# Decode attention beside a gated MLP on one core: dealing the lanes of the key and value tiles by run and then by head

## The chip, the cores and the metric

The kernel runs on one core of a Trainium2 chip. The metric is the device time of one execution in microseconds (us); lower is better. TensorE (PE in the profile, PEld its weight loads), VectorE (DVE), ScalarE (ACT) and GpSimd (POOL) compute, SyncE (SP) issues the large transfers, and sixteen DMA engines move the data from memory (HBM) into SBUF, which has 128 partitions, here also called lanes.

## The reference

One decode step for four sequences: a layer norm, an attention over a cache of 4096 keys for each of 32 heads, and a gated MLP from the same normalized input, all added to the input. Cut to what matters (the helpers that only transpose are left out):

```python
# x: (4, 1, 640); k_cache, v_cache: (4, 32, 4096, 128); wq: (640, 4096); wo: (4096, 640), all bf16
xn = _layernorm(x)
q = (xn @ wq).reshape(B, Sq, Hq, Dh)          # then (b, h, q, d)
scores = einsum('bhqd,bhkd->bhqk', q, k_cache) * Dh ** (-0.5)
p = softmax(scores)
o = einsum('bhqk,bhkd->bhqd', p, v_cache)
attn = o.reshape(B, Sq, Hq * Dh) @ wo
# gated MLP: z = gelu(xn @ w_in), halves z1 and layernorm(z2), gate from w_sp and b_sp, then @ w_out
return x + attn + mlp
```

Keys and values of one head of one sequence are 4096 x 128 values of 2 bytes, 1 MB that lies in one piece in memory.

## The kernel before

The work is cut into NT = 16 tiles: tile i is eight heads (HT = 8, head group hg = i // 4) of one sequence b = i % 4. Its keys are 8 MB that lie in one piece in memory, and its values are another 8 MB. `run_view` (line 113) deals such a piece over the 128 lanes in order: each lane holds a run of NC = 256 consecutive keys, 64 KB, and since a head has 4096 keys, LN = 16 neighbouring lanes hold one head. So lane 16 h + l holds run l of head h, and lane p starts 64 KB after lane p - 1.

`load_k` (line 134) and `load_v` (line 141) issue the transfers on SP's queue into a ring of five units of 32 KB per lane. A key tile comes as one transfer of 64 KB per lane (the first as two of 32 KB), values as transfers of one or two units, and the last unit of values in smaller cuts. The order of all loads is a list written out by hand (`plan_k`, `plan_v`, `plan_wo`), and `pump` issues the next load as soon as the instructions that read the units it overwrites have been issued; SP then waits for these readers.

For each key tile and each quarter of it, VectorE multiplies keys with the query that was spread over the lanes (`product`, line 525), folds the halves (`fold`, line 541), TensorE adds up slices through an identity matrix (`sums`, line 550), and VectorE finishes the row sums (line 564). `lane_max` (line 573) needs the maximum over a head, that is over the lanes that hold it: it lays each lane's maximum into a column by its run number (`lane_diag`) and lets a matmul with `head_scale` add up over the lanes of one head. `exps` takes the exponentials, and `deal` (line 598) writes for every lane eight copies of its probabilities, each multiplied by one column of `hmask`, so that only the copy of the lane's own head is not zero. `blocks` (line 623) multiplies them with the values, adding over all lanes; `gather` (line 641) adds the blocks up. After four tiles a head group is divided by its sums (`group_den`, `group_rden`, `group_norm`) and projected by wo (`group_turn`, `group_pick`, `group_proj`). `group_turn` moves the result into rows in which wo was loaded, and `group_pick` (line 701) selects by a mask.

The masks are built once at the start from a 128 x 128 identity (`ident_f`, line 227): `lane_diag` (line 233), `hmask` (240), `head_scale` (247), and `q_lanes` (273), which spreads a query row over the lanes of its head; `place` (289) is sixteen small GpSimd copies that put query heads in order. They stand ahead of the stretch in which the engines' order is the order of the code (`manual_schedule`, line 732).

Of the kernel before, what the change touches and what calls it, by code (L numbers as in the profile page):

```python
# [9 lines left out]
FP32 = mybir.dt.float32  # L10
BF16 = mybir.dt.bfloat16
ACT = mybir.ActivationFunctionType
ALU = mybir.AluOpType
AX = mybir.AxisListType
# [6 lines left out]
def kernel(  # L21
# [14 lines left out]
    nc = tc.nc  # L36
    P = nc.NUM_PARTITIONS
    Bsz, Sq, D = A_x.shape
    _, H, S, Dh = A_k_cache.shape
# [8 lines left out]
    HT = 8  # L48
    HG = H // HT
    NT = HG * Bsz  # L50
    LN = P // HT
    NC = HT * S // P
# [23 lines left out]
    const = ctx.enter_context(tc.tile_pool(name="const", bufs=1))  # L76
# [11 lines left out]
    def units(first, n=1):  # L88
        return ring[:, first * UNIT : (first + n) * UNIT]
# [6 lines left out]
    def pair(i):  # L96
        if i in (0, NT - 1):
            return 2 if i == 0 else V_PAIR
        return 1 if i % 2 == 0 else 0
# [12 lines left out]

    def run_view(cache, i):
        hg, b = divmod(i, Bsz)
        return cache[b, HT * hg : HT * (hg + 1)].rearrange("h s d -> (h s) d").rearrange(
            "(p c) d -> p (c d)", c=NC
        )

    w_sb = units(W_UNIT)
    w_in_sb = w_sb[:, 0 : DC * F].rearrange("p (c n) -> p c n", c=DC)  # L120
# [13 lines left out]
    def load_k(i):  # L134
        t = units(pair(i), 2)
        step = (1 if i == 0 else 2) * UNIT
        for e in reversed(range(0, 2 * UNIT, step)):
            nc.sync.dma_start(out=t[:, e : e + step], in_=run_view(A_k_cache, i)[:, e : e + step])
        k_tiles[i] = t.rearrange("p (c d) -> p c d", d=Dh)

    def load_v(i, part, unit, n):
        t = units(unit, n)
        cuts = V_CUTS if (i, part) == (NT - 1, 1) else (0, n * UC)
        for c0, c1 in zip(cuts, cuts[1:]):
            src = slice((part * UC + c0) * Dh, (part * UC + c1) * Dh)
            nc.sync.dma_start(out=t[:, c0 * Dh : c1 * Dh], in_=run_view(A_v_cache, i)[:, src])
        for e in range(n):
            v_tiles[i, part + e] = units(unit + e).rearrange("p (c d) -> p c d", d=Dh)

# [20 lines left out]
    def plan_k(i):  # L170
        plan(("k", i), pair(i), 2, load_k, i)

    def plan_v(i, part, unit, n=1):
        plan(("v", i, part), unit, n, load_v, i, part, unit, n)
# [28 lines left out]
    def pump():  # L203
        while loads:
# [21 lines left out]
    ident_f = const.tile([P, P], FP32)  # L226
# [5 lines left out]
    lane_diag = const.tile([P, LN], FP32)  # L232
    nc.vector.tensor_reduce(
        out=lane_diag[:],
        in_=ident_f[:].rearrange("p (h l) -> p l h", h=HT),
        axis=AX.X,
        op=ALU.add,
    )
    hmask = const.tile([P, HT], FP32)
    nc.vector.tensor_reduce(  # L240
        out=hmask[:],
        in_=ident_f[:].rearrange("p (h l) -> p h l", h=HT),
        axis=AX.X,
        op=ALU.add,
    )
    head_scale = const.tile([P, P], FP32)
    nc.vector.tensor_scalar(
        out=head_scale[:].rearrange("p (h l) -> p h l", h=HT),
        in0=hmask[:, :, None].to_broadcast([P, HT, LN]),
        scalar1=scale_qk,  # L250
        scalar2=None,
        op0=ALU.mult,
# [7 lines left out]
        out=sel[:],  # L260
        in_=ident_f[:].rearrange("p (g h k) -> p k h g", g=CG, k=GC),
        axis=AX.X,
        op=ALU.add,
# [3 lines left out]
        out=spread[:],  # L267
        in_=ident[:].rearrange("p (m r) -> p r m", r=HT)[:, :, None, :].to_broadcast(
            [P, HT, HT, LN]
        ),  # L270
    )
    q_lanes = const.tile([HT * Bsz, Bsz, P], BF16)
    nc.vector.tensor_copy(
        out=q_lanes[:].rearrange("r b (h l) -> r b h l", h=HT),
        in_=ident[: HT * Bsz, : HT * Bsz]
        .rearrange("r (h b) -> r b h", b=Bsz)[:, :, :, None]
        .to_broadcast([HT * Bsz, Bsz, HT, LN]),
# [2 lines left out]
    QW = CW  # L280
    QH = HT // 2
    NQG = H // QH
    place = const.tile([P, QH, HT * Bsz], BF16)
    nc.gpsimd.memset(place[:], 0.0)
    for g in range(CG):
        ps = slice(g * QW, (g + 1) * QW)
        for hh in range(QH):
            at_col = (g % 2 * QH + hh) * Bsz
            nc.gpsimd.tensor_copy(
                out=place[ps, hh, at_col : at_col + Bsz], in_=lane_diag[ps, 0:Bsz]  # L290
            )

    hmask_bf = const.tile([P, HT], BF16)
# [9 lines left out]
    for i in range(NSTAT):  # L303
# [5 lines left out]
        out=rstd[:], in_=mv[:, 1:2], func=ACT.Sqrt, bias=eps_tile[:Bsz], scale=1.0  # L309
# [4 lines left out]
        out=xn_bf[:],  # L314
        in0=x_bf[:],
# [8 lines left out]
    for c in range(DC):  # L324
        nc.tensor.transpose(  # L325
            out=xnT_ps[:, c, :], in_=xn_v[:, c, :], identity=ident[:Bsz, :Bsz]
# [11 lines left out]
    for c in range(DC):  # L338
        for hg in range(NQG):
            g = hg % CG  # L340
            nc.tensor.matmul(  # L341
                out=q_ps[hg // CG][g * QW : (g + 1) * QW, :],
# [11 lines left out]
    def out_sum(half):  # L354
        return out_ps[OG * half : OG * half + Bsz, :]

    for half in range(2):
        nc.tensor.matmul(
            out=out_sum(half),
# [339 lines left out]
    def group_pick(hg):  # L699
        own = work.tile([P, HT, HT, Bsz], FP32, name="own")  # L700
        nc.vector.tensor_tensor(
            out=own[:],
            in0=gr[hg][:],
            in1=hmask[:, None, :, None].to_broadcast([P, HT, HT, Bsz]),
            op=ALU.mult,
        )
        o_r = small.tile([P, HT, Bsz], BF16, name="o_r")
        with nc.allow_low_precision("one of the eight is the value, the others are zeros"):
            nc.vector.tensor_reduce(
                out=o_r[:],  # L710
                in_=own[:].rearrange("p r h b -> p r b h"),
                axis=AX.X,
                op=ALU.add,
            )
        gr[hg] = o_r
# [16 lines left out]
    with tc.manual_schedule(engines={E.PE, E.DVE, E.Activation, E.SP}):  # L732
# [3 lines left out]
        for i in range(NT):  # L736
# [3 lines left out]
            for n, q in enumerate(order):  # L740
# [13 lines left out]
                if ends is not None and n == 1:  # L754
                    group_rden(ends)
                    group_norm(ends)
                elif ends is not None and n == 2:
                    group_pick(ends)
# [89 lines left out]
```

## Time and profile before

| | before |
|---|---|
| median of three runs | 664.77 us (662.48 to 667.65) |
| the profiled execution: time | 664.69 us |
| the profiled execution: span from the first to the last instruction | 662.9 us |
| read from HBM | 282.24 MB, 426 GB/s over the span |
| share of the span in which the DMA engines moved SP's queue | 99.1% |
| DVE busy | 458.5 us (69%) |
| PE busy | 325.6 us (49%) |
| ACT busy | 82.6 us (12%) |
| mean granted TensorE clock | 0.727 of full speed |

The time of an execution lies a little above its span, since the span runs from the first instruction to the last. A row of a group gives the line, the engine, the operation, the tile that it writes and those that it reads, the shapes and the count, then busy time, mean duration in ns, and the idle time of the engine ahead of it with the releaser that ended most of it. A row of a stretch gives its bounds and length, the busy time of each engine in it, the granted clock, the share of time in which the DMA engines were busy, and what they moved in GB/s.

### The profile page before, as it was taken

Reading aid. Unit: us, or ns where it says so; the run is one execution under the profiler, and the core shown is the slowest. Engines: PE = TensorE matmul, PEld = TensorE weight load, DVE = VectorE, ACT = ScalarE, POOL = GpSimd, SP = SyncE. Lnnn points to the kernel's source line nnn. Section 1 sums busy time; section 2 is a strip of 40 time slices with the busy share of each in tenths; the row PEclk is TensorE's granted clock in tenths of the full one; section 3 lists DMA queues with packets and bytes.
Section 4 is the critical chain, followed back from the end, with each engine's and each line's share of the span. In section 5 each row is a group of like instructions: output and inputs, shape, how many; then the busy total and the mean of one; then the engine's idle time right before and its main releaser. Section 6 shows DMA issues by size and latency. Waiting matters only on the chain.

```text
span 662.9 us, 4934 instructions
## 1 busy us (share of the span) xinstructions
PE 325.6 (49%) x2131; PEld 149.9 (23%) x2131; DVE 458.5 (69%) x265; ACT 82.6 (12%) x202; POOL 5.6 (1%) x29
## 2 busy tenths in 40 slices
PE   0356462635546263463526447253563526457746
PEld 0114130212212132131212223121231212213334
DVE  2495975939488594966949397692957949488940
ACT  0103102020200202011020200202020020200200
POOL 2000000000000000000000000000000000000000
PEclk9765685778877677585867877577786857867886
DMA  9999999999999999999999999999999999999997
GB/s 378 437 398 395 423 458 435 443 429 427 428 439 440 423 443 432 404 463 423 439 436 435 428 443 424 431 439 428 435 436 435 435 435 436 416 429 437 423 429 282
DMA packets 8049, 282.56 MB, mean 426 GB/s; under 512 B 880, under 2 KB 2140, under 8 KB 2524
## 3 DMA queue, kind: packets, MB, share of 16 engines
q1 hardware_dynamic: 8008, 282.25, 99.1%
q8 instruction: 16, 0.26, 0.1%
q14 instruction: 5, 0.04, 0.0%
q10 hardware_dynamic: 20, 0.01, 0.0%
HBM read 282.24 MB, written 0.01 MB: 426 GB/s over the span
## 4 chain that ended last, share of the span: by engine, by line
DMA 62%; DVE 26%; PE 11%; issue 0%; ACT 0%; DVEq 0%; ACTq 0%
DMA ring<-in_A_k_cache_dram 57%; DVE ring L525 19%; PE s_ps L550 8%; DVE ring L541 6%; DMA ring<-in_A_v_cache_dram 3%; DMA ring<-in_A_wq_dram 2%; PE q_ps L341 1%; PE pv_acc L623 1%; PE pv L641 0%; PE out_ps L721 0%; DVE s_sb L564 0%; PE pv L653 0%; ACT pv_sb L637 0%; DVE m L573 0%; ACT res L816 0%
## 5 line engine op out<-in xcount | busy, mean ns | idle before, releaser
L550 PE MATMUL s_ps<-ring,ident 128*128 128x512 bf16 x624 | 212.8, 507 | 291.8 <-DVE ring L541 159.8
L525 DVE TENSOR_TENSOR ring<-ring,qbc 128x8192 bf16<-128x8192 bf16 x64 | 281.8, 4418 | 97.9 <-DMA ring<-in_A_k_cache_dram 97.9
L550 PEld LDWEIGHTS <-ident 128*128 128x128 bf16 x624 | 75.8, 122 | 413.2 <-issue 286.1
L541 DVE TENSOR_TENSOR ring<-ring 128x4096 bf16<-128x4096 bf16 x50 | 114.6, 2291 | 1.6
L623 PE MATMUL pv_acc<-ring,pm 128*32 128x512 bf16 x1008 | 68.7, 412 | 7.3 <-DMA ring<-in_A_v_cache_dram 7.3
L564 DVE TENSOR_REDUCE s_sb<-s_ps 128x64 f32<-128x512 f32 x64 | 43.8, 685 | 25.3 <-PE s_ps L550 25.3
L637 ACT COPY pv_sb<-pv_acc 128x512 f32<-128x512 f32 x16 | 9.4, 586 | 397.5 <-PE pv_acc L623 397.5
L598 ACT ACTIVATE pm<-p,hmask 128x256 bf16<-128x256 bf16 x120 | 49.5, 494 | 0.5
L623 PEld LDWEIGHTS <-pm 128*32 128x32 bf16 x1008 | 38.3, 143 | 38.6 <-issue 28.5
L583 DVE TENSOR_REDUCE nb<-max_ps 128x1 f32<-128x16 f32 x16 | 2.8, 174 | 37.0 <-PE max_ps L577 37.0
L641 PE MATMUL pv<-sel,pv_sb 128*128 128x8 f32 x128 | 17.8, 265 | 11.1 <-ACT pv_sb L637 11.1
L641 PEld LDWEIGHTS pv<-sel,pv_sb 128*128 128x128 f32 x128 | 16.3, 199 | 18.3 <-ACT pv_sb L637 18.3
L682 DVE TENSOR_TENSOR o_n<-pv,rden 128x32 bf16<-128x32 f32 x4 | 0.8, 192 | 15.9 <-PE pv L653 15.8
L575 ACT ACTIVATE lay<-lane_diag,m 128x16 f32<-128x16 f32 x16 | 4.9, 309 | 47.6 <-DVE m L573 47.6
L587 ACT ACTIVATE p<-s_sb,nb 128x256 bf16<-128x256 f32 x16 | 8.1, 508 | 19.5 <-DVE nb L583 19.5
L577 PE MATMUL max_ps<-lay,head_scale 128*128 128x16 f32 x32 | 6.3, 272 | 3.7 <-ACT lay L575 3.7
L511 ACT CAST q_rows<-qr_ps 32x128 bf16<-32x128 f32 x4 | 1.0, 256 | 51.8 <-PE qr_ps L503 51.8
L665 POOL TENSOR_TENSOR own_sum<-acc,hmask 128x32 f32<-128x32 f32 x4 | 2.0, 500 | 621.1 <-ACT p L587 621.1
L573 DVE TENSOR_REDUCE m<-s_sb 128x1 f32<-128x256 f32 x16 | 6.7, 420 | 0.5
L341 PE MATMUL q_ps<-ring,xnT 128*32 128x512 bf16 x40 | 4.5, 631 | 3.9 <-DMA ring<-in_A_wq_dram 3.9
L577 PEld LDWEIGHTS max_ps<-lay,head_scale 128*128 128x128 f32 x32 | 5.0, 199 | 5.6 <-ACT lay L575 5.6
L325 PE MATMUL xnT_ps<-ident,xn_bf 4*128 4x4 bf16 x5 | 0.4, 178 | 11.5 <-DVE xn_bf L313 11.5
(90 smaller groups left out, 74.6 us busy)
## 6 DMA issues: line engine op xcount, KB each, us to landing
ring<-in_A_v_cache_dram SPq DMA_DIRECT2D x7, 4096.0 KB, 23.6
ring<-in_A_k_cache_dram SPq DMA_DIRECT2D x2, 4096.0 KB, 29.2
ring<-in_A_wq_dram SPq DMA_DIRECT2D x1, 5120.0 KB
wo<-in_A_wo_dram SPq DMA_DIRECT2D x3, 1280.0 KB, 25.9
ring<-in_B_w_in_dram SPq DMA_DIRECT2D x1, 2160.0 KB, 38.4
ring<-in_A_v_cache_dram SPq DMA_DIRECT2D x1, 2048.0 KB, 20.5
ring<-in_A_v_cache_dram SPq DMA_DIRECT2D x1, 1024.0 KB, 22.2
ring<-in_A_v_cache_dram SPq DMA_DIRECT2D x2, 512.0 KB
```

The costliest lines, as they stand in the source:

```text
L341: nc.tensor.matmul(out=q_ps[hg // CG][g * QW : (g + 1) * QW, :], lhsT=xnT[:, c, :], rhs=wq_sb[:, c, hg * QH * Dh : (hg + 1) * QH * Dh], st ...
L525: nc.vector.tensor_tensor(out=t, in0=t, in1=qbcs[i // Bsz][:, i % Bsz, None, :].to_broadcast([P, QC, Dh]), op=ALU.mult,)
L541: nc.vector.tensor_tensor(out=t[:, :, 0:HD2], in0=t[:, :, 0:HD2], in1=t[:, :, HD2:Dh], op=ALU.add)
L550: nc.tensor.matmul(out=s[:], lhsT=ident[:], rhs=t[:, :, g * RW : (g + 1) * RW], start=(g == 0), stop=(g == n - 1),)
L564: nc.vector.tensor_reduce(out=scores[i][:, q * QC : (q + 1) * QC], in_=sums_ps.pop((i, q))[:], axis=AX.X, op=ALU.add,)
L573: nc.vector.tensor_reduce(out=m1[:], in_=scores[i][:], axis=AX.X, op=ALU.max)
L577: nc.tensor.matmul(out=ps[:], lhsT=head_scale[:], rhs=d[:], start=True, stop=True)
L587: nc.scalar.activation(out=p[:], in_=scores.pop(i)[:], func=ACT.Exp, bias=nb[:], scale=scale_qk, accum_out=acc[hg % NACC][:, b : b + 1],)
L598: nc.scalar.activation(out=p_m[i % 2][:, :, h, :], in_=probs[i][:].rearrange("p (n c) -> p n c", c=BC), func=ACT.Copy, scale=hmask[:, h : ...
L623: nc.tensor.matmul(out=pv_acc[g * CW : (g + 1) * CW, :], lhsT=pm[:, n, :, :].rearrange("p h (k c) -> p c (h k)", k=GC)[:, c, :], rhs=v_nat ...
L637: nc.scalar.copy(out=pv_sb[:], in_=pv_acc[:])
L641: nc.tensor.matmul(out=pvs[hg][:, :, b], lhsT=pv_sb[:, k * Dh : (k + 1) * Dh], rhs=sel[:, k, :], start=(k == 0), stop=stop and k == GC - 1,)
```

## The change

Lane 8 l + h now holds run l of head h. Neighbouring lanes belong to different heads, whose data lie 1 MB apart, and lanes that are eight apart hold neighbouring runs, 64 KB apart. The view of the caches becomes three-dimensional (16 runs, 8 heads, the bytes of a run), and each load cuts its last dimension. Everything that depends on which lane holds which head follows: `lane_diag`, `hmask`, `head_scale` and `q_lanes` exchange the order of h and l. `group_pick` selects rows of wo's order and not of the caches', so it keeps the old pattern under a new name, `rmask`. `place` had used `lane_diag` as a small diagonal; it now reads the diagonal from `ident_f`.

```diff
     def run_view(cache, i):
         hg, b = divmod(i, Bsz)
-        return cache[b, HT * hg : HT * (hg + 1)].rearrange("h s d -> (h s) d").rearrange(
-            "(p c) d -> p (c d)", c=NC
-        )
+        return cache[b, HT * hg : HT * (hg + 1)].rearrange("h (l c) d -> l h (c d)", c=NC)
...
-            nc.sync.dma_start(out=t[:, e : e + step], in_=run_view(A_k_cache, i)[:, e : e + step])
+            nc.sync.dma_start(out=t[:, e : e + step], in_=run_view(A_k_cache, i)[:, :, e : e + step])
...
-            nc.sync.dma_start(out=t[:, c0 * Dh : c1 * Dh], in_=run_view(A_v_cache, i)[:, src])
+            nc.sync.dma_start(out=t[:, c0 * Dh : c1 * Dh], in_=run_view(A_v_cache, i)[:, :, src])
...
     nc.vector.tensor_reduce(
         out=lane_diag[:],
-        in_=ident_f[:].rearrange("p (h l) -> p l h", h=HT),
+        in_=ident_f[:].rearrange("p (l h) -> p l h", h=HT),
...
     hmask = const.tile([P, HT], FP32)
     nc.vector.tensor_reduce(
         out=hmask[:],
+        in_=ident_f[:].rearrange("p (l h) -> p h l", h=HT),
+        axis=AX.X,
+        op=ALU.add,
+    )
+    rmask = const.tile([P, HT], FP32)
+    nc.vector.tensor_reduce(
+        out=rmask[:],
         in_=ident_f[:].rearrange("p (h l) -> p h l", h=HT),
...
-        out=head_scale[:].rearrange("p (h l) -> p h l", h=HT),
-        in0=hmask[:, :, None].to_broadcast([P, HT, LN]),
+        out=head_scale[:].rearrange("p (l h) -> p l h", h=HT),
+        in0=hmask[:, None, :].to_broadcast([P, LN, HT]),
...
-        out=q_lanes[:].rearrange("r b (h l) -> r b h l", h=HT),
+        out=q_lanes[:].rearrange("r b (l h) -> r b h l", h=HT),
...
-                out=place[ps, hh, at_col : at_col + Bsz], in_=lane_diag[ps, 0:Bsz]
+                out=place[ps, hh, at_col : at_col + Bsz], in_=ident_f[ps, g * QW : g * QW + Bsz]
...
-            in1=hmask[:, None, :, None].to_broadcast([P, HT, HT, Bsz]),
+            in1=rmask[:, None, :, None].to_broadcast([P, HT, HT, Bsz]),
```

## The prediction

> **What bounds the kernel now.** I read the page first, from its span down to the memory rate, then the stretches of time, and last the chain and the queue's own waits.
>
> ```profile
> span 662.9 us, 4934 instructions
> ...
> PE 325.6 (49%) x2131; PEld 149.9 (23%) x2131; DVE 458.5 (69%) x265; ACT 82.6 (12%) x202; POOL 5.6 (1%) x29
> ...
> DMA  9999999999999999999999999999999999999997
> GB/s 378 437 398 395 423 458 435 443 429 427 428 439 440 423 443 432 404 463 423 439 436 435 428 443 424 431 439 428 435 436 435 435 435 436 416 429 437 423 429 282
> ...
> q1 hardware_dynamic: 8008, 282.25, 99.1%
> ...
> HBM read 282.24 MB, written 0.01 MB: 426 GB/s over the span
> ```
>
> The busiest engine, DVE, works 69% of the span; the sixteen DMA engines are busy 99.1% of it with SP's queue. So the time is bytes divided by rate. K and V are 2 x 4 x 32 x 4096 x 128 x 2 bytes = 268.4 MB of the 282.24 MB. The change cannot alter the bytes; it can only alter the rate at which K and V arrive. Single slices of the GB/s row swing because a packet is counted where it starts, so I asked for longer stretches (columns: length, busy time of PE, PEld, DVE, ACT, POOL, then granted clock, DMA share, GB/s):
>
> ```profile
> 25.00:50.00 25.00, 10.18 (x25) 3.51 (x26) 24.05 (x9) 0.00 (x0) 0.00 (x0) 0.57 1.00 412
> 54.00:74.00 20.00, 8.61 (x44) 3.71 (x43) 13.10 (x25) 7.49 (x16) 0.00 (x0) 0.50 0.96 392
> 74.00:100.00 26.00, 15.68 (x103) 6.88 (x101) 21.34 (x12) 1.19 (x3) 0.00 (x0) 0.83 1.02 438
> 100.00:320.00 220.00, 102.81 (x628) 45.94 (x629) 156.75 (x76) 28.63 (x74) 0.24 (x1) 0.71 1.00 434
> 320.00:600.00 280.00, 138.37 (x858) 62.04 (x858) 200.06 (x102) 33.66 (x86) 0.48 (x2) 0.72 1.00 433
> 600.00:643.00 43.00, 28.96 (x215) 14.50 (x214) 33.35 (x21) 6.30 (x16) 1.28 (x1) 0.90 1.00 430
> ```
>
> Two things are to be seen. From 100 to 600 us the rate stands at 433 to 434 GB/s, with no drift, while lanes are 64 KB apart in memory. And from 54 to 74 us, while the second K tile comes in, it is 392 GB/s with the engines still called 96% busy: a slow transfer looks busy, so the busy share would not show a loss of rate; GB/s does.
>
> The chain of waits says the same: 57% of it is the arrival of K. First two of the queue's issues in order of time, then the chain in order of time, around one of them and at its end (start, length, what):
>
> ```profile
> 120.32 0.33 SPq L138 DMA_DIRECT2D ring<-in_A_k_cache_dram  x1
> 136.74 0.33 SPq L146 DMA_DIRECT2D ring<-in_A_v_cache_dram  x1
> ```
>
> ```profile
> 120.32 25.93 DMA ring<-in_A_k_cache_dram
> ...
> 630.79 20.51 DMA ring<-in_A_v_cache_dram
> 651.30 0.04 issue
> ```
>
> An 8 MB tile (8.39 million bytes) needs 8.39 / 0.434 = 19.3 us; it lands 25.9 us after its issue. So each load is issued some 6.6 us before the engines turn to it, and that lead covers everything SP does. After the last V piece lands at 651.30 the kernel needs 662.9 - 651.3 = 11.6 us to its end.
>
> **The change, part by part.**
>
> 1. *Masks at the start.* One VectorE reduction is added (rmask); the others keep their sizes and swap contiguous and strided views. The nearest rows, from the readers of ident_f and from the page's groups:
>
> ```profile
> L233 DVE TENSOR_REDUCE lane_diag<-ident_f x1: 348/348/348, 12.5 to 12.5; 128x16 f32<-128x128 f32 x1
> L240 DVE TENSOR_REDUCE hmask<-ident_f x1: 263/263/263, 12.8 to 12.8; 128x8 f32<-128x128 f32 x1
> ```
>
> ```profile
> L341 PE MATMUL q_ps<-ring,xnT 128*32 128x512 bf16 x40 | 4.5, 631 | 3.9 <-DMA ring<-in_A_wq_dram 3.9
> ```
>
> lane_diag and hmask are the strided and the contiguous form: 348 and 263 ns. So rmask costs 0.26 us, hmask turned strided at most 0.1 more, and q_lanes, which now writes with a stride of 8, between its 0.41 us of now and the pace of the strided spread copy (1.06 us for 1024 columns, so 0.53 for 512). Sum: 0.26 to 0.5 us. VectorE's last piece there, the copy of xnT, is over by 13.94 us, and TensorE then waits for wq, which lands at 16.11: over 2 us of cover. Without it this would be 0.5 us once. POOL's sixteen small copies of place start when ident_f is there (11.58) and no longer behind lane_diag (12.85): 1.3 us earlier, but their reader runs at 20.97, so nothing. On the path: 0.
>
> 2. *The later readers of the masks.* group_pick reads rmask in place of hmask, same shape, 0.41 us three times. deal, lane_max, blocks and group_den run the same instructions on permuted lanes. Nothing.
>
> 3. *The issue of a load.* The source now counts 16 x 8 rows and no longer 128. An issue of K or V takes 0.33 us on SP; the dearest shape in the trace, w_in, takes 0.79. Forty issues would then be 0 to 40 x 0.46 = 18.4 us of SP in all, but singly 0.46 us inside a lead of 6.6. On the path: 0; without the lead 0.46 us a load. No edit adds a wait, and the order of loads stays.
>
> 4. *The reads themselves.* This is the term that decides. Every packet stays one run of up to 64 KB. What moves is the address: neighbouring lanes were 64 KB apart and are now 1 MB apart within groups of eight. If each DMA engine serves eight neighbouring lanes, as the change's words suppose (no view shows the assignment), the sixteen engines were 512 KB apart and stand 64 KB apart; each then steps by 1 MB. The trace has no load of that pattern. Bounds: the best sustained row is 434 GB/s, so no gain in the bulk; the worst row is 392. At 392, K and V take 268.4 / 0.392 = 684.7 us against 268.4 / 0.434 = 618.4: up to +66 us. At the other end, the stretch of 392 itself could vanish: 20 x (1 - 392/434) = 1.9 us gained. I take 0, by the row it is nearest to: some forty loads of widely different shapes (64 KB, 32 KB, and wq and w_in with other row lengths) pass through the 433 to 434 GB/s rows or close to them, and only one K tile is slow though all have the same spacing. So spacing alone does not set the rate here; the engines' own pace seems to. [...]
>
> **Sum.** 662.9 us of span + 0 + 0 + 0 + 0 = 662.9. The profiled execution's own time is 664.69, 1.8 us above its span, and the median is 664.77: the forecast is 664.7, with 659 to 668 as its own range (the slow stretch gone and a little more, or met twice).
>
> **Rivals.**
>
> *A. The new pattern collides in memory (slower).* Place: every K and V load. Engines that work in step ask for addresses that differ only by multiples of 64 KB, then of 1 MB, and if these meet in one part of the memory, packets stretch. For it: the stretch from 54 to 74 us shows that this kernel's reads can drop 10% with nothing else changed in the queue. Against it: all loads before were powers of two apart too, and held 434. Price: all at 392 gives 664.7 + 66 = 731; a third of the bytes, 664.7 + 22 = 687. It decides as soon as a tenth of the bytes is hit (6.6 us). Chance 0.30, of which 0.20 up to 687. [...]
>
> *B. The split over DMA engines changes.* With 16 rows outermost at the source and 128 lanes at the destination, the engines may be given other lanes than now, and two of them may write through one path at a time. If pairs then share, the 434 becomes 217: 618 us more, some 1283 us. For it: no load in the trace has unequal outer counts, so nothing shows this split. Against it: the change only makes sense if the split is by eight lanes either way. Chance 0.04. [...]
>
> *C. The losses of the start go (faster by over 1%).* It needs 6.65 us. Against 434 GB/s the stretches lose 25 x (1 - 412/434) = 1.3 us from 25 to 50, 1.9 from 54 to 74, 0.4 from 600 to 643; before 25 us (wq) nothing is touched. That is 3.6 us, so 661: still within 1%, even if all of it went. Only a bulk rate of 439 or more would do it, and no long row shows that. Chance 0.07, mostly for what the rows do not show.
>
> *D. It does not do what it says,* the engines' spacing being other than supposed: the time is the forecast's, and it belongs there.
>
> **How the numbers follow.** Within 1% (658.1 to 671.4, about what a measurement of this kernel can tell from no change, since its three runs spread from 662.48 to 667.65): the forecast, with D, 0.59. Slower by over 1%: A and B, 0.34. Faster: C, 0.07. The range must leave out no more than 0.2: below 658, most of C, 0.05; above 687, the heavy part of A (0.10) and B (0.04). So 658 to 687.
>
> **What would show it right or wrong.** Right: 433 to 434 GB/s between 100 and 600 us, K tiles landing 25 to 26 us after issue, the same chain with 57% K, one more reduction on VectorE near 13 us, wq still the releaser of the first matmuls. Step 3 is wrong if SP's issues of K grow and the lead falls towards nothing. Step 4 is wrong if the long rows leave 434: 390 and landings near 28 us say A, about 217 says B, 440 or more says C. The slow stretch vanishing with the rest unchanged would say that spacing caused it, and be worth 1.9 us.

## The result and the profile after

The changed kernel takes 1331.43 us (median; 1326.96 to 1332.63) against 663.65 us for the kernel before: a ratio of 2.003, 95% interval 1.993 to 2.013. The forecast was 664.7 us, range 658 to 687, so it was wrong by a factor of two. The page after, the rows that answer to those of before:

```profile
span 1328.7 us, 4934 instructions
...
PE 354.0 (27%) x2131; PEld 158.7 (12%) x2131; DVE 459.7 (35%) x266; ACT 82.6 (6%) x202; POOL 6.8 (1%) x29
...
DMA  9999999999999999999999999999999999999998
GB/s 283 259 218 196 226 219 197 216 211 200 213 197 221 201 210 217 223 199 221 198 213 211 200 217 200 215 221 201 213 208 207 211 203 216 206 207 209 217 212 192
...
q1 hardware_dynamic: 8008, 282.25, 99.6%
...
HBM read 282.24 MB, written 0.01 MB: 212 GB/s over the span
```

The same bytes in the same 8008 packets, the DMA engines as busy as before (99.6%), VectorE as busy in microseconds (459.7 after 458.5): only the GB/s row has changed, and it has halved. The stretches after (same columns as before):

```profile
25.00:50.00 25.00, 3.21 (x8) 1.18 (x9) 12.59 (x4) 0.59 (x1) 0.00 (x0) 1.00 1.02 212
100.00:320.00 220.00, 59.90 (x332) 24.97 (x332) 84.30 (x39) 10.53 (x27) 0.00 (x0) 0.59 1.00 211
600.00:1200.00 600.00, 162.09 (x906) 70.36 (x906) 217.46 (x109) 34.51 (x88) 0.48 (x2) 0.61 1.00 209
```

The loss is there from the first K tile on and stays even; only the stretch from 54 to 74 us, in which the MLP's w_in lands, reads higher (317 GB/s). At 210 GB/s K and V, 268.4 MB, take 268.4 / 0.210 = 1278 us where they took 618, 660 us more; the span grew by 1328.7 - 662.9 = 665.8. So, to within the rounding of the rate, the rate of K and V is the whole loss. The waits show who pays, VectorE's product standing before each K tile; first its row of the page before, which ends with 97.9 us of waiting, then its wait after:

```profile
L525 DVE TENSOR_TENSOR ring<-ring,qbc 128x8192 bf16<-128x8192 bf16 x64 | 281.8, 4418 | 97.9 <-DMA ring<-in_A_k_cache_dram 97.9
```

```profile
DVE ring L530 <- DMA ring<-in_A_k_cache_dram: 474.6, 17, 38.9
```

The masks and SP's issues, from the readers of ident_f, from the row of q_lanes and from the loads' own row:

```profile
L231 DVE TENSOR_REDUCE lane_diag<-ident_f x1: 267/267/267, 12.4 to 12.4; 128x16 f32<-128x128 f32 x1
L238 DVE TENSOR_REDUCE hmask<-ident_f x1: 358/358/358, 12.6 to 12.6; 128x8 f32<-128x128 f32 x1
L245 DVE TENSOR_REDUCE rmask<-ident_f x1: 264/264/264, 12.9 to 12.9; 128x8 f32<-128x128 f32 x1
```

```profile
L278 DVE COPY q_lanes<-ident x1: 1276/1276/1276, 13.5 to 13.5; 32x512 bf16<-32x512 bf16 x1
```

```profile
L136 SPq DMA_DIRECT2D ring<-in_A_k_cache_dram x17: 536/537/1067, 1.2 to 1132.8; - x17
...
DMA to landing us min/median/max: 36.0/67.4/68.2
```

An issue of K costs 0.54 us and no longer 0.33, and a load lands 67 us after its issue; 8.39 / 0.211 = 39.8 us of it is the transfer, so the lead is now 27 us: the queue, 99.6% busy, is not short of work.

### The profile page after: what moved, and what is told of

Read it like the earlier page. It is cut to its first block, busy times and chain, and to the rows that moved or that the text cites. A ratio compares the mean times of both kernels' runs of the same rounds, so it can differ in the third digit from the quotient of the medians.

```text
span 1328.7 us, 4934 instructions
## 1 busy us (share of the span) xinstructions
PE 354.0 (27%) x2131; PEld 158.7 (12%) x2131; DVE 459.7 (35%) x266; ACT 82.6 (6%) x202; POOL 6.8 (1%) x29
## 3 DMA queue, kind: packets, MB, share of 16 engines
q1 hardware_dynamic: 8008, 282.25, 99.6%
## 4 chain that ended last, share of the span: by engine, by line
another core or an unknown queue 52%; DVE 22%; PE 15%; DMA 9%; issue 1%; ACT 1%; SPq 0%; DVEq 0%; ACTq 0%
DVE ring L530 15%; PE s_ps L555 7%; DMA ring<-in_A_v_cache_dram 6%; PE pv_acc L628 6%; DVE ring L546 6%; DMA ring<-in_A_k_cache_dram 3%; PE pv L646 1%; DVE s_sb L569 1%; ACT pv_sb L642 1%; PE out_ps L726 1%; PE max_ps L582 0%; DVE nb L588 0%; PE pv L658 0%; DVE rden L682 0%
## 5 line engine op out<-in xcount | busy, mean ns | idle before, releaser
L628 PE MATMUL pv_acc<-ring,pm 128*32 128x512 bf16 x1008 | 92.8, 530 | 298.0 <-DMA ring<-in_A_v_cache_dram 298.0
L628 PEld LDWEIGHTS <-pm 128*32 128x32 bf16 x1008 | 46.2, 151 | 340.9 <-issue 335.7
```

The lines of the kernel that those rows point to most:

```text
L628: nc.tensor.matmul(out=pv_acc[g * CW : (g + 1) * CW, :], lhsT=pm[:, n, :, :].rearrange("p h (k c) -> p c (h k)", k=GC)[:, c, :], rhs=v_nat ...
```

## The experiments

Three explanations stood at first, suppositions that no view shows. **Write paths:** the source's shape (16 outer steps) changes which lanes a DMA engine serves, and engines that run at the same time get in each other's way where they write into SBUF. **Read addresses:** the new spacing in memory (64 KB between engines, 1 MB within one) collides. **Issue:** a transfer with three dimensions, or with the longer issue, is slow by itself. The kernel before ran beside the experiments in 662.2 to 664.6 us. Only the kernels of e8 and e9 were timed several times (four and ten); every other time below is that of one execution.

### The new shape with the old addresses (e1_shape16)

```diff
-        return cache[b, HT * hg : HT * (hg + 1)].rearrange("h s d -> (h s) d").rearrange(...)
+        return bass.AP(cache.tensor, (b * H + HT * hg) * S * Dh,
+                       [[7 * NC * Dh, LN], [NC * Dh, HT], [1, NC * Dh]])
```

> Before's masks and lane order; only the source view of the K and V loads is written as 16 blocks of 8 runs, the blocks starting 7 runs (448 KB) apart instead of 8, so that it cannot be folded into 128 equal steps. Lanes read almost the addresses of before (some runs are read twice, the last ones not, so the attention is over other keys). Write-path theory (the 16 outer steps change the lanes that an engine serves, and engines then share a write path into SBUF): the rate halves to about 210 GB/s, 1300 to 1340 us. Read-address theory (64 KB between engines and 1 MB within one collide in memory): neither spacing is here, 660 to 670 us. Issue theory (a transfer of three dimensions is slow by itself): 1300 to 1340 us.

Measured: 1330.75 us. The stretches of this kernel:

```profile
100.00:320.00 220.00, 60.74 (x332) 25.18 (x332) 84.36 (x39) 10.66 (x27) 0.00 (x0) 0.60 1.00 211
```

The shape alone, with the masks of before and with runs that lie next to each other in memory, gives the whole loss to within a microsecond. The addresses are not needed for it.

### The old shape with far addresses (e2_pitch1m)

```diff
+        return bass.AP(cache.tensor, i * NC * Dh, [[S * Dh, P], [1, NC * Dh]])
```

> Before's masks; the source view keeps 128 outer steps, but each step is 1 MB: lane p of tile i reads run i of head p of the whole cache, so neighbouring lanes are 1 MB apart everywhere (the attention mixes heads). Write-path theory: 128 outer steps on both sides, so 660 to 670 us. Read-address theory: 1 MB steps inside an engine and multiples of 1 MB between engines, slower than before by at least a few per cent and up to 1330 us. Issue theory: two dimensions as before, 660 to 670 us.

Measured: 673.43 us beside 662.35, between the two ranges on record: above the 660 to 670 of the write paths and below the few per cent of the read addresses.

```profile
100.00:320.00 220.00, 99.97 (x610) 44.23 (x610) 149.43 (x73) 28.18 (x72) 0.24 (x1) 0.69 1.00 424
320.00:600.00 280.00, 134.07 (x862) 61.29 (x861) 199.69 (x103) 34.49 (x88) 0.48 (x2) 0.74 1.00 432
```

A lane pitch of 1 MB costs 11 us, 1.7% (1.8% of the 618 us of K and V): 424 and 432 GB/s where it was 434 and 433. By this one run, read addresses have a price, but it is a sixtieth of the loss.

### Plain transfers of half the lanes (e3_halves)

```diff
+            for p0 in (0, P // 2):
+                ps = slice(p0, p0 + P // 2)
+                nc.sync.dma_start(out=t[ps, e : e + step], in_=run_view(A_k_cache, i)[ps, e : e + step])
```

> Before's masks, lanes, addresses and two-dimensional views; each K and V load is issued as two, lanes 0 to 63 and lanes 64 to 127. Computes the reference. Write-path theory: if a transfer of 64 lanes reaches only half of the write paths, both halves run at half the rate, one after the other on every engine: about 217 GB/s, 1270 to 1340 us. Read-address theory: the addresses are before's, 660 to 675 us. Issue theory: twice as many issues of 0.33 us inside a lead of 6.6 us, 660 to 675 us.

Measured: 1335.92 us, 208 to 210 GB/s from 100 us on.

```profile
100.00:320.00 220.00, 56.97 (x312) 23.33 (x316) 83.58 (x38) 10.22 (x26) 0.00 (x0) 0.61 1.00 210
```

Nothing is left of the change here: two-dimensional views, old addresses, old lanes. Apart from twice as many issues, only the lanes that one transfer writes differ, 64 neighbouring ones instead of all 128. The rate is 210 GB/s where it was 434. That speaks for the writing side; by what path a lane is written, no view shows.

### Three dimensions with 128 outer steps (e4_outer128)

```diff
+                out=t[:, e : e + step].rearrange("p (a n) -> p a n", a=2),
+                in_=bass.AP(v.tensor, v.offset, [[NC * Dh, P], [h - h // 4, 2], [1, h]]),
```

> Before's masks and lanes; each K and V load has three dimensions on both sides, 128 lanes of two pieces, the second piece of the source starting a quarter of a piece early so that it cannot be folded (some keys are read twice, others not). Packets are half as long. Write-path theory: 128 outer steps on both sides, 660 to 670 us. Read-address theory: 660 to 670 us. Issue theory (three dimensions by themselves): about 1330 us.

Measured: 663.60 us, 432 GB/s. Three dimensions cost nothing (662.35 us beside it). The longer issue remained as a form of the issue explanation, since the slow kernels so far all had issues of about 0.5 us (0.54 in the change and in e1, 0.56 in e3), and this one 0.37.

### The mask edits alone (e5_masks)

Against the changed kernel:

```diff
-        return cache[b, HT * hg : HT * (hg + 1)].rearrange("h (l c) d -> l h (c d)", c=NC)
+        return cache[b, HT * hg : HT * (hg + 1)].rearrange("h s d -> (h s) d").rearrange(
+            "(p c) d -> p (c d)", c=NC
+        )
```

> All the mask edits of the change, but the K and V loads and their lanes as before (so the masks name other heads than the lanes hold). Every theory: the mask edits cost at most 0.5 us, covered by the wait for wq; 660 to 667 us. If it is above 671 the masks have a part in the loss.

Measured: 662.40 us. The masks have no part in it.

### Sixteen neighbouring lanes at a time (e6_lanes16)

```diff
+            for p0 in range(0, P, LN):
+                ps = slice(p0, p0 + LN)
+                nc.sync.dma_start(out=t[ps, e : e + step], in_=run_view(A_k_cache, i)[ps, e : e + step])
```

> Before's masks, lanes and addresses; each K and V load is issued as eight transfers of 16 neighbouring lanes. Computes the reference. [...] Issue theory in a second form (it is not the shape but the longer issue, 0.54 us against 0.33, that goes with the slow rate in the change and in the halves): if these issues take 0.33 us, 660 to 690 us. Read-address theory, already weak: 16 runs in one 1 MB stretch at a time, so engines 64 KB apart as the change meant, about 1330 us.

Measured: 2318.5 us. Its stretches, and its K loads:

```profile
320.00:600.00 280.00, 37.38 (x231) 16.25 (x228) 47.62 (x25) 10.22 (x26) 0.24 (x1) 0.56 1.01 116
600.00:1200.00 600.00, 84.95 (x485) 36.27 (x486) 118.57 (x59) 19.60 (x50) 0.24 (x1) 0.55 1.00 116
```

```profile
L140 SPq DMA_DIRECT2D ring<-in_A_k_cache_dram x136: 310/311/859, 1.2 to 2071.6; - x136
```

116 GB/s is 27% of 434, with all engines busy and issues of 0.31 us, the shortest of all. So the rate falls without the longer issue, and the fewer neighbouring lanes one plain transfer holds, the slower: 128 give 434, 64 give 209, 16 give 116. The write-path theory was given a quarter, 108 GB/s and 2500 to 2700 us, an estimate of the author that no run before had shown; the time lies below that range, and no run shows why.

### Thirty-two outer steps of four lanes (e7_shape32)

```diff
+        return bass.AP(cache.tensor, (b * H + HT * hg) * S * Dh,
+                       [[3 * NC * Dh, 32], [NC * Dh, 4], [1, NC * Dh]])
```

> Before's masks; source view of 32 blocks of 4 runs, blocks 3 runs apart so that it cannot be folded (some runs are read twice). [...] Issue theory: about 1330 us. Read-address theory: 660 to 670 us.

Measured: 662.41 us. The write-path theory had been given either 1300 to 1340 us or 660 to 670.

```profile
100.00:320.00 220.00, 103.68 (x629) 46.22 (x630) 159.13 (x77) 26.66 (x68) 0.24 (x1) 0.71 1.00 434
```

```profile
L140 SPq DMA_DIRECT2D ring<-in_A_k_cache_dram x17: 534/535/1097, 1.2 to 568.8; - x17
```

An issue as long as the change's (0.54 us), a view that cannot be folded either, and the full rate. So neither the issue nor the third dimension is the cause: with four lanes on one outer step the shape is harmless (434 GB/s), with eight it halves the rate (211 in e1). Why it does is not shown: no view tells which lanes an engine serves.

### Near reads in the old shape (e8_near), and the change's aim in a good shape (e9_fours)

e8 gives each lane four quarter runs, 16 KB from lane to lane. e9 keeps runs whole and repairs the change: lane 64 a + 4 l + j holds run l of head 2 j + a, with masks to match (left out here). The first diff is against the kernel before, the second against the changed kernel.

```diff
+                out=t[:, e : e + step].rearrange("p (a n) -> p a n", a=4),
+                in_=bass.AP(v.tensor, v.offset + e * P, [[q, P], [q * P, 4], [1, q]]),
```

> The aim of the change without its shape: 128 outer steps on both sides, but each lane holds four quarter runs, and lanes are 16 KB apart in the source (64 KB for every fourth lane), so that one round of all lanes reads one close stretch of 2 MB; all bytes of a tile are read once. Masks as before (lanes mix heads). Packets are a quarter as long. Write-path theory: full rate, and if closeness in memory brings nothing, 662 to 672 us (four times the packets may cost up to 1%); if closeness helps, below 660 us. Read-address theory: near spacing collides, clearly slower, up to 1330 us.

```diff
-        return cache[b, HT * hg : HT * (hg + 1)].rearrange("h (l c) d -> l h (c d)", c=NC)
+        return cache[b, HT * hg : HT * (hg + 1)].rearrange("(j a) (l c) d -> (a l) j (c d)", a=2, c=NC)
```

> The change's aim in a shape that keeps groups of four: lane 64 a + 4 l + j holds run l of head 2 j + a, so the source counts 32 outer steps of 64 KB and 4 inner steps of 2 MB, and every group of four lanes starts 64 KB after the one before. Masks to match; it computes the reference. Write-path theory: 32 outer steps ran at full rate, so about 434 GB/s and 660 to 667 us; since nearer reads brought nothing, not below 658. Read-address theory: engines 64 KB apart with steps of 2 MB, as in the change, 1330 us.

Measured: e8 666.79 us, ratio to the kernel before 1.0065 (1.0049 to 1.0082), with, by its edit, pieces a quarter as long for K and V; e9 662.36 us, ratio 0.9996 (0.9987 to 1.0006). The stretch of e9:

```profile
100.00:320.00 220.00, 103.40 (x629) 46.10 (x630) 159.08 (x77) 26.64 (x68) 0.24 (x1) 0.71 1.00 434
```

So the aim itself, groups of four lanes that start 64 KB apart, can be had at full rate, and brings nothing: 434 GB/s is what the engines give either way. Read addresses are done with as a cause of the halving, and no version here beats the kernel before.

### Moving the engines apart in time (e10_pieces, e11_skew1, e12_skew2)

It matters how many neighbouring lanes one plain transfer holds (434, 209 and 116 GB/s for 128, 64 and 16). Two explanations were left, both the author's suppositions: two engines **share** a path while they meet on it, or an engine is **slow by itself** whenever it writes lanes that are not its own in the plain transfer. e10 issues lower and upper halves in turn, in pieces of 16 KB a lane; e11 and e12 add one and two extra transfers that are meant to hold up half of the engines, one to put them out of step with the others, two to bring them back into step. Sharing was given 1270 to 1340 us in e10, 670 to 720 us in e11 and 1270 to 1340 us in e12, estimates of the author from 434 GB/s and half of it; slow by itself was given 1270 to 1340 us in all three.

```diff
+            for q0 in range(e, e + step, UNIT // 2):
+                for p0 in (0, P // 2):
+                    ps, qs = slice(p0, p0 + P // 2), slice(q0, q0 + UNIT // 2)
+                    nc.sync.dma_start(out=t[ps, qs], in_=run_view(A_k_cache, i)[ps, qs])
...
+        for g in range(1):  # e12: range(2)
+            nc.sync.dma_start(
+                out=ring[8 * g : 8 * g + 8, 3 * UNIT // 2 : 2 * UNIT],
+                in_=A_k_cache[0, 0, 512 * g : 512 * (g + 1)].rearrange("(p c) d -> p (c d)", p=8))
```

> The two halves (lanes 0 to 63, 64 to 127) in pieces of 16 KB a lane, lower and upper in turn; base for the next two. Computes the reference. [...]

> [...] Slow-by-itself variant: nothing changes, 1270 to 1340 us.

> [...] Slow-by-itself variant: 1270 to 1340 us.

Measured: 1237.84, 1261.73 and 1297.50 us. e10 lies below the range that both explanations gave it, and e12 inside. The extra transfer of e11 did not help at all: 670 to 720 us was what the sharing theory as I had written it asked for, and 1261.73 is 8 us below the range of the other explanation. By itself this does not decide: no view shows whether half of the engines was held up, or which engines meet, if any do.

### Lanes eight apart, and two engines alone (e13_stride8, e14_two)

```diff
+            for j in range(HT):
+                nc.sync.dma_start(out=t[j::HT, e : e + step], in_=run_view(A_k_cache, i)[j::HT, e : e + step])
```

> Before's masks, lanes and addresses; each K and V load is issued as eight transfers of 16 lanes that are eight apart (lanes j, j + 8, j + 16, ...), where the kernel with eight transfers of 16 neighbouring lanes took 2318.5 us. Computes the reference. [...] Slow-by-itself variant (an engine is slow whenever it writes other lanes than in the plain 128-lane transfer): most engines write other lanes in both kernels, so about 2300 us as with neighbouring lanes, or no clear reason for a difference.

Measured: 1943.43 us, a miss for both in the time: sharing was given 1240 to 1340 us, the author's estimate from half of 434 GB/s. A long stretch, one in which a load was under way, and the longest of SP's own waits:

```profile
600.00:1200.00 600.00, 94.89 (x606) 43.22 (x607) 141.95 (x73) 24.29 (x62) 0.24 (x1) 0.57 0.69 144
930.00:960.00 30.00, 0.00 (x0) 0.00 (x0) 0.00 (x0) 0.00 (x0) 0.00 (x0) 0.50 1.02 210
```

```profile
SPq L150 <- DVE ring L547: 809.8, 17, 53.2
SPq L139 <- DVE ring L547: 673.8, 14, 53.0
```

Over the long stretch the DMA engines are busy only 69% of the time, which no kernel so far had shown (in e6 it was 100%). The waits tell why: before it issues the next load, SP stands for up to 53 us until a fold of VectorE is done. VectorE itself works 142 of the 600 us, and from 930 to 960 us, while a load is under way, no engine computes at all. So loading and computing take turns. That lengthens the time and has nothing to do with the rate; why the strided lanes bring these waits was not tested. From 930 to 960 us the engines are all busy and move 210 GB/s: about half of 434, as the sharing theory had it, where 16 neighbouring lanes gave 116. So the theory had the rate right, and the time was missed because the loads no longer overlap with the work.

```diff
+            if i == 2:
+                v = bass.AP(v.tensor, v.offset, [[63 * NC * Dh, 2], [NC * Dh, P // 2], [1, step]])
```

> As before, but the K load of tile 2 alone has a source of 2 outer steps of 64 runs (63 runs apart, so that it cannot be folded; some keys of that tile are others), which puts it on two DMA engines that each write 64 lanes one after the other, nearly all of them other lanes than theirs in the plain transfer, one in each half of the lanes. Sharing theory: the two never meet, so each packet takes its 2.42 us: the load lands some 155 us after the engines turn to it, and the kernel takes 780 to 830 us. Slow-by-itself variant: packets of about 5 us, landing after some 310 us, 930 to 990 us. If the load goes over other than two engines, its landing says so (over sixteen: 20 to 40 us).

Measured: 815.14 us, inside the 780 to 830 that the sharing theory gave. The stretches around that load, which was issued at 80.54 and waited for until 256.75 us:

```profile
95.00:130.00 35.00, 1.58 (x18) 1.19 (x10) 0.17 (x1) 4.69 (x12) 0.00 (x0) 0.58 0.98 238
105.00:125.00 20.00, 0.00 (x0) 0.00 (x0) 0.00 (x0) 0.00 (x0) 0.00 (x0) 0.50 0.96 197
...
150.00:225.00 75.00, 0.00 (x0) 0.00 (x0) 0.00 (x0) 0.00 (x0) 0.00 (x0) 0.50 0.12 54
```

From 150 to 225 us an eighth of the engines, two of sixteen, is busy and moves 54 GB/s, which is 434 x 2 / 16. By the edit these two write all 128 lanes, most of which a plain load, with all sixteen busy, must leave to the others; yet they move their full share: an engine is not slow by itself. Slow-by-itself falls. But while the next V load (issued at 95.34, a plain one of 128 steps) ran beside it, all sixteen together gave 238 GB/s at 98% busy from 95 to 130 us, and 197 at 96% from 105 to 125: less than half of 434 there.

## Why the prediction was wrong, point by point

**The bound and its reading: right.** Time is bytes by rate, the rate shows in GB/s and not in the busy share, and the loss is K and V's rate alone. The warning that a slow transfer looks busy came true to the letter: 99.1% before, 99.6% after.

**Steps 1 and 2, the masks: right on the path, one size wrong.** rmask takes 0.264 us (forecast 0.26), hmask in the strided form 0.358, lane_diag in the contiguous one 0.267. But q_lanes takes 1.276 us, where 0.41 to 0.53 was forecast from the spread copy, so the masks cost 0.264 + 0.095 - 0.081 + 0.869 = 1.15 us of VectorE and not 0.26 to 0.5. The wait for wq covers this too: e5 shows 662.40 us for all mask edits together.

**Step 3, the issue: right in size and in effect.** 0.54 us, between the 0.33 and 0.79 named; e7 runs at full rate with it.

**Step 4, the reads: the step that failed.** It put the term at 0 and at worst at +66 us; K and V took some 660 us more. Its premise, that what moves is the address, was wrong: e1 has the whole loss with nearly the old addresses, and e9 moves the addresses and loses nothing. What moved the time was the shape of the source, 16 steps of eight lanes (211 GB/s in e1, where 32 steps of four kept 434 in e7). It was given the bounds 434 and 392 GB/s, and 0 was taken because loads of widely different shapes held the rate. But the shapes differed only in the length of a run. In every one of them the same number of lanes stood outermost at the source and at the destination, and the rows could not bound a load that broke this. The text saw it ("no load in the trace has unequal outer counts") and put it under rival B, yet kept 392 as the worst end of the step. An operation that no row shows has no worst row.

**Rival B: the price was right, the mechanism fits and was not seen, the chance was wrong.** It said that engines given other lanes may write through one path at a time, 217 GB/s and some 1283 us; measured were 209 to 212 GB/s and 1331 us, and the long rows near 217 were the sign named for B. That plain transfers of 64 lanes (e3, 208 to 210 GB/s) and of 16 lanes eight apart (e13, 210 while a load is under way) also run at half the rate speaks for a shared path and does not show one; which lanes meet in the 16 x 8 form was not seen, and e11, at 1261.73 us, did not bear out the sharing theory as it was written. It got 4 in 100 with one argument against it, that the change only makes sense if the split stays. That is an argument from intent, and no evidence: no row of the trace showed that a source with steps of eight lanes is split as one with 128 steps is, and the text beside it said so.

**Rival A:** far reads do cost, 1.7% at 1 MB in e2, but in the change nothing that can be seen beside the halving; e1 has the loss without them. **Rival C:** its bound held, no kernel went above 434 GB/s in a long stretch. **Rival D** fell with the time itself, which is not the forecast's; and e9 shows that where groups of four lanes do start 64 KB apart, nothing is gained.

**The slow stretch** from 54 to 74 us (392 GB/s) is not set by the spacing alone: with the same loads in e5 it is 420. It differs from kernel to kernel (382 in e2, 430 in e4), and its cause stays open.

## What to carry to other kernels

When a load is rearranged at its source, look at how many outer steps source and destination have and how many neighbouring lanes hang on one step: 128 steps, or 32 steps of four lanes, kept 434 GB/s here, 16 steps of eight lanes or plain transfers of 64 lanes halved it (208 to 212 GB/s), and plain transfers of 16 neighbouring lanes left about a quarter (116). The loss did not show in the busy share of the DMA engines (99.1% before, 99.6% after), only in GB/s. And if a forecast meets an operation without a row, the range must reach to the rival that names what is new about it.

## What the hardware showed unexpectedly

A load that two engines carried cost not only its own time: beside a plain load all sixteen engines together fell to 197 GB/s at 96% busy (e14, 105 to 125 us; 238 over the whole of that load), where 434 was kept in the long stretches before. Why all sixteen slow down stays open. Whether the extra transfer of e11 was of no use for the same reason is not shown; no run tests it alone. Which lanes each engine serves in the 16 x 8 form was not seen either, only what it costs: 209 to 212 GB/s.
